# A two-layer mixture of experts on one core: weighting expert 0 in the first pass of the down phase, in place of the second

## The chip, the core and the metric

The kernel runs on one core of a Trainium2 chip. TensorE (PE) multiplies matrices into PSUM; VectorE (DVE), ScalarE (ACT) and GpSimd (POOL) work beside it, and DMA queues of SyncE (SP) and POOL move data between HBM and SBUF. Every engine takes its instructions in order. The metric is the time of one execution on the device in microseconds.

## The reference

Three stages follow one another: an attention, a mixture of experts with one expert a token, and a second mixture in which all eight experts see every token and their results are added, weighted with a matrix P. The change touches only the last product of the third stage.

```python
def _moe2_ref(x, w_gate, w1, w2):          # N, D, E, F = 2304, 512, 8, 1024
    logits = x @ w_gate
    logits = logits - logits.max()
    P = np.exp(logits)
    for _ in range(8):
        P /= P.sum(1, keepdims=True) + 1e-09
        P /= P.sum(0, keepdims=True) + 1e-09
        P *= N / E
    out = np.zeros((N, D), dtype=np.float32)
    for e in range(E):
        h = np.maximum(x @ w1[e], 0.0)
        ye = h @ w2[e]
        out += P[:, e:e + 1] * ye
```

## The kernel before

The third stage has an up phase (x @ w1) and a down phase (h @ w2). Both cut their matrices into 2 x 2 quadrants and form the product from seven block products instead of eight, on sums and differences of quadrants. Blocks are numbered b = 0 to 6. For h the seven operands are: b 0 is h11, b 2 is h12 - h11, b 3 is h22 - h12, b 1 is h22 - h12 + h11, b 4 is h21, b 6 is h22, and b 5 is h21 less the operand of b 1. An operand in float32 is split into a rounded part (a cast on ACT, L939) and the remainder (a subtraction on DVE, L943), and a block product consists of three products of these parts.

The tokens are taken in NU = 3 parts of UN = 384 (times two for the quadrants). In the up phase `up` (L1143 ff.) multiplies the quadrants of h by P for the experts 1 to 7, combines them and saves the seven operands in `hd[e, u, b]` in HBM. For expert 0 P isn't known yet at that time (it is computed while expert 0 runs), so its four quadrants are saved unweighted in the places of b 0, 2, 4 and 6.

The down phase is one loop over 168 products n. Its order is the table `STEPS`: two passes (experts 1, 2, 3, 4, then 5, 6, 7, 0), in each the blocks in the order 0, 3, 1, 2, 4, 6, 5, in each block the four experts, and for each of these the three parts u. So a pass has 84 products, and a block round has 12. Expert 0 is last of its round, but in block 5 of the second pass it is first. A product is 24 matmuls of 128x384 (L1446) into the PSUM bank of its part; after the fourth expert of a round, DVE adds the bank into the quadrants of the result (`merge`, one to four additions of 128x768, at most two of them a product). Tile names: `df` holds four stages of 768 KB for h and some W2 quadrants, `xa` and `w1c` the rounded parts and remainders, `dg`, `wr` and the pad of `x` (x2) the other W2 quadrants, `pbx` rows of P; `rA` to `rD` are the four banks, `kept` is the identity.

What is issued behind the matmuls of product n, in this order:

- `h_make(n + 3)`: the operand of the product three further on is cast and split; then `h_load` asks SP for the next stages. For expert 0 `h_make` also loads a second block (`SRC`) into the next stage, combines the two on DVE (L1325, L1331, L1333), multiplies by P (L1328, `p_load` fetches P), and in four blocks stores what later blocks need (L1335, from POOL's queue).
- `w_make(m + 1)`, once in three products: a sum of two W2 quadrants on DVE for the blocks 3, 1, 2 and 6, then its cast and its remainder.
- merges, then the loads of W2 quadrants (`w_load`).

In block 5 of the second pass finished rows leave as well: `put` transposes them on PE (L1399) into a bank, ACT copies them, and POOL writes them out by an indirect DMA (L1404).

Of the kernel before, what the change touches and what calls it, by code (L numbers as in the profile page):

```python
# [97 lines left out]
def _program(ctx, tc, qT, kT, vv, tau, wg, mod, mbias, cst, wA, wg2, wU, wD, out):  # L98
# [678 lines left out]
    def experts(es):  # L777
# [450 lines left out]
        def gates():  # L1228
# [21 lines left out]
        PASS = ((1, 2, 3, 4), (5, 6, 7, 0))  # L1250
        DORD = (0, 3, 1, 2, 4, 6, 5)
        STEPS = [(i, b, e) for i, es4 in enumerate(PASS) for b in DORD
                 for e in (es4 if (i, b) != (1, 5) else es4[3:] + es4[:3])]
        NM = len(STEPS)
        SEQ = [(m, u) for m in range(NM - 2) for u in range(NU)] + [(m, u) for u in range(NU) for m in (NM - 2, NM - 1)]
        NB = len(SEQ)
        SRC = {0: (0,), 3: (6, 2), 1: (3, 0), 2: (2, 0), 4: (4,), 6: (6,), 5: (4, 1)}
        LOADS = [(n, b) for n, (m, u) in enumerate(SEQ)
                 for b in (SRC[STEPS[m][1]] if STEPS[m][2] == 0 else STEPS[m][1:2])]
        FIRST = {}  # L1260
        for i, (n, _) in enumerate(LOADS):
            FIRST.setdefault(n, i)
        SCALED = [n for n, (m, u) in enumerate(SEQ) if STEPS[m][2] == 0 and STEPS[m][1] in (0, 3, 2, 4, 6)]
        NST = 4
        loaded = [0]

        def open_down():
            xb_s.close()
            df = es.enter_context(pool_l("df")).tile([P, N_X], F32, name="df")
            D["stage"] = [cut(df, N_T * i, 4, UN) for i in range(NST)]  # L1270
            D["w"] = [[cut(xa, 2048 * j + 1024 * i, 4, 256) for i in range(2)] for j in range(2)]
            D["h"] = [[cut(t, lo + N_T * i, 4, UN) for i in range(2)]
                      for t, lo in ((xa, 4096), (xa, 4096 + 2 * N_T), (w1c, 0), (w1c, 2 * N_T))]
            at = NST * N_T
            D["blk"] = {(j, 0): cut(df, at + 1024 * j, 4, 256) for j in range(4)}
            D["o"] = [cut(df, at + 1024 * i, 2, 512) for i in range(4)]

        def open_rest():
            xc_s.close()
            dg = es.enter_context(tc.tile_pool(name="dg", bufs=1, side="right", reuse_waits="tile")).tile(  # L1280
                [P, N_X], F32, name="dg")
            room = [cut(dg, 1024 * i, 4, 256) for i in range(10)] + [cut(wr, 0, 4, 256), pad]
            D["blk"].update(((j, i), room.pop(0)) for i in (2, 3, 1) for j in range(4))

        def w_load(i, j, k):
            nc.sync.dma_start(out=D["blk"][j, k],
                              in_=wD[PASS[i][j], :, 1024 * k:1024 * k + 1024].rearrange("p (k n) -> p k n", k=4))

        def w_make(m):
            if m >= NM:  # L1290
                return
            i, b, e = STEPS[m]
            j = PASS[i].index(e)
            w11, w12, w21, w22 = (D["blk"][j, k] if (j, k) in D["blk"] else None for k in range(4))
            if b == 3:
                op2(V, w21, w11, w21, ALU.subtract)
            elif b == 1:
# [1 line left out]
            elif b == 2:  # L1299
                op2(V, w11, w21, w11, ALU.add)  # L1300
            elif b == 6:
                op2(V, w12, w12, w21, ALU.subtract)
            both(D["w"][m % 2], {0: w11, 3: w21, 1: w21, 2: w11, 4: w12, 6: w12, 5: w22}[b], A, V)

        def h_load(n):
            top = FIRST.get(n, len(LOADS)) + NST
            while loaded[0] < min(top, len(LOADS)):
                k, b = LOADS[loaded[0]]
                m, u = SEQ[k]
                nc.sync.dma_start(out=D["stage"][loaded[0] % NST], in_=hd[STEPS[m][2], u, b])  # L1310
                loaded[0] += 1

        def p_load(i):
            if i < len(SCALED):
                load_p(pbs[i % 2], 0, SEQ[SCALED[i]][1])
# [24 lines left out]
        for n in range(n_up):  # L1340
# [96 lines left out]
        for n, (m, u) in enumerate(SEQ):  # L1437
# [12 lines left out]
            if m < NM - 3:  # L1450
                if u == 0:
                    w_make(m + 1)
            elif m == NM - 3:
                if u:
                    w_make(m + u)
            if last:
                merge(i, b, u, q[u][:, :, 0:UN])
            for _ in range(min(2, len(pend))):
# [3 lines left out]
            elif i == 0 and u == 2:  # L1462
                if b == 4:
                    w_load(1, j, 0)
                elif b == 5:
                    w_load(1, j, 2)
                    w_load(1, j, 1)
                    if j == 0:
                        p_load(0)
                        p_load(1)  # L1470
            elif (i, b) == (1, 0) and u == 2:
                w_load(1, j, 3)
            if (i, b) == (1, 5):
# [112 lines left out]
```

## Time and profile before

| | us |
|---|---|
| runs shown (3) | 2038.81, 2039.24, 2040.8; median 2039.24 |
| profiled execution | 2038.46 |
| its span, first to last instruction | 2036.7 |
| PE busy in the span | 1982.0 |
| DVE busy in the span | 1555.2 |
| down phase, first product to last instruction | 1294.4 to 2036.7 |

The times of the profile count from the span's start. A matmul that stands in the queue behind another counts as busy PE, so the length of a stretch against the number of products in it says more than PE's busy share. The granted clock of TensorE is given as a share of full speed (2.4 GHz); the lower level is 1.2 GHz. The first product of the second pass, number 84, starts at 1643.85 us.

### The profile page before, as it was taken

To read this page: it belongs to the slowest core of one execution; us is meant where nothing else is said; L and a number is where in the kernel's file an instruction comes from. 1 tells how busy PE (TensorE), PEld (TensorE's weight loads), DVE (VectorE), ACT (ScalarE), POOL (GpSimd) and SP (SyncE) were. 2 spreads that over 40 slices of the span, in tenths; PEclk is the share of its full clock that TensorE was granted. 3 is DMA by queue.
4 is the path that set the end of the run, shared out by engine and by line. 5 is a ranking of instruction groups with operands and counts; after the bars stand their busy time and mean duration, and the time that the engine had idled before them with its cause. 6 is when DMAs were issued, how large, how long until landed. Compare 5 with 4: busy or idle time off the path is not lost.

```text
span 2036.7 us, 32533 instructions
## 1 busy us (share of the span) xinstructions
PE 1982.0 (97%) x12677; PEld 1906.8 (94%) x12677; DVE 1555.2 (76%) x1957; ACT 870.6 (43%) x1152; POOL 483.7 (24%) x395
## 2 busy tenths in 40 slices
PE   8999998999998999999999999999999999999997
PEld 7877777999978999999999999999999999989997
DVE  7888886656566799999999999867766568778772
ACT  6777763555554322222222222454444443334433
POOL 6564625042002133323233323100000000000004
PEclk9999998999999999999999999999999999999999
DMA  5232324566523566677767676985565777767763
GB/s 188 84 123 100 100 66 155 194 224 198 187 92 107 177 236 233 230 254 252 242 232 238 228 251 235 398 300 188 186 212 205 256 269 257 277 238 255 260 228 120
DMA packets 177215, 421.13 MB, mean 207 GB/s; under 512 B 16396, under 2 KB 126364, under 8 KB 177052
## 3 DMA queue, kind: packets, MB, share of 16 engines
q1 hardware_dynamic: 170700, 399.03, 56.8%
q0 software_dynamic: 4928, 19.93, 2.6%
q8 instruction: 102, 1.67, 0.3%
q14 instruction: 61, 0.50, 0.1%
q10 hardware_dynamic: 1424, 0.01, 0.0%
HBM read 274.91 MB, written 143.99 MB: 206 GB/s over the span
## 4 chain that ended last, share of the span: by engine, by line
PE 58%; issue 7%; DVE 2%; ACT 1%; DMA 1%; POOL 0%; POOLq 0%; ACTq 0%; DVEq 0%; SPq 0%
PE qB L1136 10%; PE qC L1136 10%; PE qA L1136 9%; PE rA L1446 7%; PE rD L1446 6%; PE rB L1446 6%; PE rC L1446 6%; PE qD L1136 4%; DVE df L946 1%; ACT xa L939 1%; DVE xa L943 1%; DMA df<-hd 0%; DMA hd<-df 0%; ACT w1c L939 0%; DVE x L946 0%
## 5 line engine op out<-in xcount | busy, mean ns | idle before, releaser
L943 DVE TENSOR_TENSOR xa<-df,xa 128x1536 fp32r<-128x1536 f32 (+1 forms) x100 | 166.2, 1670 | 88.8 <-ACT xa L939 88.7
L946 POOL TENSOR_TENSOR x<-x 128x768 f32<-128x768 f32 x45 | 115.0, 2555 | 443.2 <-DVE x L1140 349.5
L939 ACT CAST xa<-df 128x1536 fp32r<-128x1536 f32 (+1 forms) x100 | 139.9, 1412 | 156.1 <-DVE df L946 66.2
L943 DVE TENSOR_TENSOR w1c<-df,w1c 128x1536 fp32r<-128x1536 f32 x84 | 147.4, 1756 | 72.1 <-ACT w1c L939 70.3
L946 DVE TENSOR_TENSOR x<-x 128x768 f32<-128x768 f32 x135 | 196.3, 1454 | 4.5
L939 ACT CAST w1c<-df 128x1536 fp32r<-128x1536 f32 x84 | 124.4, 1482 | 160.2 <-DVE df L946 55.8
L1335 POOL DMA_DIRECT2D hd<-df x12 | 6.6, 549 | 594.3 <-DVE df L946 594.3
L1136 PE MATMUL qB<-xc,w1c 128*128 128x384 f32 x768 | 143.7, 335 | 2.9 <-DVE x L946 1.9
L1136 PE MATMUL qC<-xa,w1c 128*128 128x384 f32 x768 | 144.0, 335 | 1.5 <-ACT x L1192 1.5
L1136 PE MATMUL qA<-xb,w1c 128*128 128x384 f32 x768 | 144.4, 336 | 0.2 <-ACT x L1192 0.2
L478 DVE TENSOR_REDUCE cols<-s 128x1 f32<-128x576 f32 x144 | 103.9, 754 | 44.6 <-PE s L473 43.6
L1136 PEld LDWEIGHTS qB<-xc,w1c 128*128 128x128 f32 x768 | 133.9, 188 | 3.5 <-issue 2.2
L1136 PEld LDWEIGHTS qA<-xb,w1c 128*128 128x128 f32 x768 | 134.5, 189 | 2.8 <-issue 2.2
L1136 PEld LDWEIGHTS qC<-xa,w1c 128*128 128x128 f32 x768 | 133.7, 188 | 1.8 <-ACT x L1192 1.8
L489 ACT ACTIVATE sa<-s,cols 128x576 f32<-128x576 f32 x144 | 102.6, 741 | 64.2 <-DVE cols L478 64.1
L1140 DVE SCALAR_TENSOR_TENSOR x<-x,pbx 128x768 f32<-128x768 f32 x126 | 125.8, 999 | 4.3
L473 PE MATMUL s<-colr 128*128 128x288 f32 x640 | 107.2, 309 | 6.5 <-DVE cols L500 2.5
L172 DVE TENSOR_TENSOR colr<-cols,colr 128x1024 fp32r<-128x1024 f32 x57 | 71.5, 1258 | 54.7 <-ACT colr L171 54.5
L473 PEld LDWEIGHTS s<-colr 128*128 128x128 f32 x640 | 88.9, 189 | 16.4 <-issue 10.7
L1446 PE MATMUL rA<-xa 128*128 128x384 f32 x576 | 104.0, 335 | 0.0
L946 DVE TENSOR_TENSOR x<-qD,x 128x768 f32<-128x768 f32 x84 | 80.0, 952 | 31.2 <-ACT x L1186 16.8
L1446 PE MATMUL rD<-w1c,xa 128*128 128x384 f32 x552 | 101.2, 338 | 0.0
(299 smaller groups left out, 4460.3 us busy)
## 6 DMA issues: line engine op xcount, KB each, us to landing
df<-hd SPq DMA_DIRECT2D x180, 768.0 KB, 4.5
hd<-x SPq DMA_DIRECT2D x317, 384.0 KB, 3.2
cols<-wA SPq DMA_DIRECT2D x84, 512.0 KB, 4.5
pbx<-pd SPq DMA_DIRECT2D x114, 192.0 KB, 5.3
wr<-wU SPq DMA_DIRECT2D x16, 768.0 KB, 6.2
dg<-wD SPq DMA_DIRECT2D x20, 512.0 KB, 6.9
hd<-df POOLq DMA_DIRECT2D x12, 768.0 KB, 7.3
cols<-qT SPq DMA_DIRECT2D x15, 576.0 KB, 3.8
```

Of the source, the lines that this page charges most:

```text
L172: sub.tensor_tensor(out=lo[i], in0=raw, in1=hi[i].bitcast(F32), op=ALU.subtract)
L473: mm(s[:, hf, 0:288], lhsT=l, rhs=r, start=n == 0, stop=n == len(ops) - 1)
L478: V.tensor_reduce(out=mx[:, i % 18:i % 18 + 1], in_=St[i][:, :, 0:288], axis=AX.XY, op=ALU.max, negate=True)
L489: A.activation(out=e.rearrange("p (h c) -> p h c", h=2), in_=St[i][:, :, 0:288], func=AF.Exp, bias=mxs[i // 18 % 2][0][:, i % 18:i % 18 + 1])
L939: A.copy(out=out, in_=in_)
L943: sub.tensor_tensor(out=hi_lo[1], in0=src, in1=hi_lo[0].bitcast(F32), op=ALU.subtract)
L946: eng.tensor_tensor(out=out, in0=x, in1=y, op=op)
L1136: mm(q[:, i, 0:UN], lhsT=a[l][:, k, 128 * i:128 * i + 128], rhs=b[r][:, k], start=first and k == 0 and j == 0, stop=k == nk - 1 and j == 2 ...
L1140: V.scalar_tensor_tensor(out=out, in0=src, scalar=0.0, in1=bc(pv.unsqueeze(1), [P, n, UN]), op0=ALU.max, op1=ALU.mult)
L1335: G.dma_start(out=hd[0, u, b], in_=x)
L1446: mm(q[u][:, i2, 0:UN], lhsT=a[l][:, k, 128 * i2:128 * i2 + 128], rhs=h[r][:, k], start=first and k == 0 and j == 0, stop=last and k == 3 ...
```

## The change

Expert 0 is no longer weighted and combined when its operands are due. A new function, `weigh0(n)`, does so in the first pass, in 12 groups of six products (n = 12 to 83): a group takes one part u and one of the four column blocks k of a quadrant (128x384, 192 KB). It loads the four quadrants in its first two products (SP), multiplies them by P, forms the combinations, eight DVE operations in its fourth, fifth and sixth product, and stores the seven operands from POOL's queue. Its five small tiles `D["p"]` lie in `df`, `wr`, `pbx` (two) and `dg`. `h_make` treats expert 0 like the others; `STEPS` has it last in block 5 as well. Apart from that, the sum of W2 quadrants is taken out of `w_make` into `w_sum`, which is called at the second product of a step for the step after the next, so ahead of its cast. (A step is the three products of one expert and block.)

```diff
-                 for e in (es4 if (i, b) != (1, 5) else es4[3:] + es4[:3])]
+                 for e in es4]
...
+            D["p"] = [df[:, at + 4096:at + 4096 + UN], wr[:, 1024:1024 + UN], pbs[1][0], pbs[1][1]]
...
+            D["p"].append(dg[:, 10240:10240 + UN])
...
         def h_make(n):
             if n < NB:
-                m, u = SEQ[n]
-                _, b, e = STEPS[m]
-                x = D["stage"][FIRST[n] % NST]
-                if e == 0:
-                    y = D["stage"][(FIRST[n] + 1) % NST]
-                    if b == 3:
-                        op2(V, x, x, y, ALU.subtract)
-                    if n in SCALED:
-                        i = SCALED.index(n)
-                        op2(V, x, x, bc(pbs[i % 2][0 if b in (0, 4) else 1].unsqueeze(1), [P, 4, UN]), ALU.mult)
-                        p_load(i + 2)
-                    if b == 1:
-                        op2(V, x, x, y, ALU.add)
-                    elif b in (2, 5):
-                        op2(V, x, x, y, ALU.subtract)
-                    if b in (0, 3, 1, 4):
-                        G.dma_start(out=hd[0, u, b], in_=x)
-                both(D["h"][n % 4], x, A, V)
+                both(D["h"][n % 4], D["stage"][n % NST], A, V)
                 h_load(n + 1)
+
+        def weigh0(n):
+            gr, s = divmod(n - 12, 6)
+            if not 0 <= gr < 4 * NU:
+                return
+            u, k = divmod(gr, 4)
+            h11, h12, h21, h22, t1 = D["p"]
+            pv = pbs[0]
+            src = lambda b: hd[0, u, b, :, k]
...
+            def scale(x, t, b=None):
+                op2(V, x, x, pv[t], ALU.mult)
+                if b is not None:
+                    G.dma_start(out=src(b), in_=x)
+
+            def comb(out, x, y, op, b):
+                op2(V, out, x, y, op)
+                G.dma_start(out=src(b), in_=out)
+
+            if s == 0:
+                if k == 0:
+                    load_p(pv, 0, u)
+                load(h12, 2)
+                load(h22, 6)
+            elif s == 1:
+                load(h11, 0)
+                load(h21, 4)
+            elif s == 3:
+                scale(h11, 0, 0)
+                scale(h12, 1)
+                comb(t1, h12, h11, ALU.subtract, 2)
+            elif s == 4:
+                scale(h22, 1, 6)
+                comb(h12, h22, h12, ALU.subtract, 3)
+            elif s == 5:
+                comb(h11, h12, h11, ALU.add, 1)
+                scale(h21, 0, 4)
+                comb(t1, h21, h11, ALU.subtract, 5)
...
             if m < NM - 3:
                 if u == 0:
                     w_make(m + 1)
+                elif u == 1:
+                    w_sum(m + 2)
             elif m == NM - 3:
                 if u:
                     w_make(m + u)
+            weigh0(n)
```

On DVE, three places show what moved. The first is the end of block 1's round in the first pass, products 33 to 35. Before (L943 of 128x1536 is the remainder of h, with which a product's list begins; 128x1024 is W2, `x_3583` the merges):

```order
L943 TENSOR_TENSOR xa<-df,xa 128x1024
L946 TENSOR_TENSOR x_3583<-rC,x_3583 128x2x384 x2
L943 TENSOR_TENSOR xa<-df,xa 128x1536
L946 TENSOR_TENSOR x_3583<-rC,x_3583 128x2x384
L946 TENSOR_TENSOR x_3583<-rB,x_3583 128x2x384
L943 TENSOR_TENSOR w1c<-df,w1c 128x1536
L946 TENSOR_TENSOR x_3583<-rB,x_3583 128x2x384 x2
```

And now, at the same place:

```order
L943 TENSOR_TENSOR xa<-df,xa 128x1024
L946 TENSOR_TENSOR df<-df,pbx 128x384
L946 TENSOR_TENSOR wr<-wr,pbx 128x384
L946 TENSOR_TENSOR dg<-wr,df 128x384
L946 TENSOR_TENSOR x_3583<-rC,x_3583 128x2x384 x2
L943 TENSOR_TENSOR xa<-df,xa 128x1536
L946 TENSOR_TENSOR df<-dg,df 128x1024
L946 TENSOR_TENSOR pbx<-pbx 128x384
L946 TENSOR_TENSOR wr<-pbx,wr 128x384
L946 TENSOR_TENSOR x_3583<-rC,x_3583 128x2x384
L946 TENSOR_TENSOR x_3583<-rB,x_3583 128x2x384
```

Ahead of the merges stand three operations of expert 0 in one product, and a W2 sum and two operations in the next.

The second place is in the second pass, expert 0 in block 3, the W2 sum of the block that follows among its rows. Before:

```order
L946 TENSOR_TENSOR df<-df 128x1536
L946 TENSOR_TENSOR df<-df,pbx 128x1536
L943 TENSOR_TENSOR xa<-df,xa 128x1536
L946 TENSOR_TENSOR dg<-df,dg 128x1024
L943 TENSOR_TENSOR xa<-dg,xa 128x1024
L946 TENSOR_TENSOR df<-df 128x1536
L946 TENSOR_TENSOR df<-df,pbx 128x1536
L943 TENSOR_TENSOR w1c<-df,w1c 128x1536
```

And now the same stretch, between the last merges of block 0 and the sums for block 1:

```order
L943 TENSOR_TENSOR w1c<-df,w1c 128x1536
L946 TENSOR_TENSOR dg<-df,dg 128x1024
L943 TENSOR_TENSOR xa<-df,xa 128x1536 x2
L943 TENSOR_TENSOR xa<-dg,xa 128x1024
L943 TENSOR_TENSOR w1c<-df,w1c 128x1536
```

The combinations and multiplications of 128x1536 are gone, and the W2 sum stands two rows of h ahead of the remainder that needs it, not right ahead of it.

The third place is SP's queue in the first pass, which before held only the loads of h (L1310) there. Now a group's four loads stand among those of the other experts:

```order
L1312 DMA df<-hd 128x1536 x5
L1330 DMA wr<-hd 128x384
L1330 DMA pbx<-hd 128x384
L1312 DMA df<-hd 128x1536
L1330 DMA df<-hd 128x384
L1330 DMA pbx<-hd 128x384
```

Behind the two pairs, the experts' loads of 768 KB go on in the same queue.

## Rows read from the trace of the kernel before

**Rows 1.** The page, part 1: busy time, share of the span, instructions.

```profile
PE 1982.0 (97%) x12677; PEld 1906.8 (94%) x12677; DVE 1555.2 (76%) x1957; ACT 870.6 (43%) x1152; POOL 483.7 (24%) x395
```

**Rows 2.** Stretches of the down phase: length, busy time by engine, granted clock, DMA.

```profile
1294.41:1643.85 349.44, 349.44 (x2018) 349.44 (x2017) 232.43 (x165) 154.53 (x118) 2.56 (x1) 1.00 0.67 241
...
1697.93:1703.83 5.90, 4.32 (x25) 4.03 (x25) 4.73 (x6) 3.80 (x3) 0.00 (x0) 1.00 0.93 372
...
1741.58:1749.31 7.73, 4.44 (x24) 4.12 (x24) 4.66 (x4) 2.58 (x3) 0.00 (x0) 1.00 0.91 299
1749.31:1755.15 5.84, 5.84 (x25) 5.84 (x25) 5.84 (x6) 2.63 (x2) 0.00 (x0) 0.71 0.76 290
...
1796.75:1805.95 9.20, 4.38 (x25) 4.06 (x24) 4.57 (x4) 2.56 (x3) 0.00 (x0) 0.91 0.78 268
1805.95:1812.60 6.65, 6.64 (x24) 6.64 (x25) 6.65 (x7) 4.28 (x3) 0.00 (x0) 0.61 0.93 358
...
1845.88:1857.91 12.03, 8.78 (x49) 8.14 (x48) 8.73 (x7) 2.99 (x3) 0.00 (x0) 1.00 0.60 220
1857.91:1863.78 5.87, 5.87 (x24) 5.87 (x25) 5.87 (x5) 3.65 (x3) 0.00 (x0) 0.71 0.72 263
...
1967.78:1974.26 6.48, 4.33 (x25) 4.00 (x24) 4.86 (x5) 3.89 (x4) 0.00 (x0) 1.00 0.64 243
1974.26:1980.93 6.67, 6.67 (x32) 6.67 (x33) 6.16 (x4) 3.87 (x4) 2.58 (x4) 0.74 0.96 350
```

**Rows 3.** Timeline, start and length in us; in brackets idle time before and releaser.

```profile
1793.27 1.76 DVE L946 TENSOR_TENSOR df<-df 128x1536 f32<-128x1536 f32 x1 [3.01 <-DMA df<-hd]
1795.14 1.48 ACT L939 CAST w1c<-df 128x1536 fp32r<-128x1536 f32 x1 [6.67 <-DVE df L946]
...
1800.09 1.47 ACT L939 CAST xa<-df 128x1536 fp32r<-128x1536 f32 x1 [3.47 <-DMA df<-hd]
...
1803.27 1.22 DVE L946 TENSOR_TENSOR df<-dg,df 128x1024 f32<-128x1024 f32 x1
...
1805.95 6.81 PE L1446 MATMUL rC<-xa 128*128 128x384 f32 x24 [4.82 <-ACT xa L939]
```

**Rows 4.** Groups of DVE in the down phase: busy us, mean ns | idle before.

```profile
L943 DVE TENSOR_TENSOR w1c<-df,w1c 128x1536 fp32r<-128x1536 f32 x84 | 147.4, 1756 | 72.1 <-ACT w1c L939 70.3 <-PE rD L1446 1.6 <-PE rA L1446 0.2
...
L946 DVE TENSOR_TENSOR df<-df,pbx 128x1536 f32<-128x1536 f32 x15 | 26.3, 1754 | 0.1
L946 DVE TENSOR_TENSOR df<-df 128x1536 f32<-128x1536 f32 x12 | 21.0, 1753 | 3.1 <-DMA df<-hd 3.0
L946 DVE TENSOR_TENSOR x<-rB,x 128x768 f32<-128x768 f32 x20 | 18.6, 953 | 6.3 <-PE rB L1446 6.2
```

**Rows 5.** Groups of DVE in the whole span, the forms nearest to 128x384.

```profile
L946 DVE TENSOR_TENSOR x<-x 128x768 f32<-128x768 f32 x135 | 196.3, 1454 | 4.5
...
L943 DVE TENSOR_TENSOR w1c<-wr,w1c 128x512 fp32r<-128x512 f32 x75 | 51.7, 689 | 15.4 <-ACT w1c L939 15.4
...
L811 DVE SCALAR_TENSOR_TENSOR late<-p,late 128x256 fp32r<-128x256 f32 x80 | 32.9, 420 | 29.7 <-ACT late L810 29.4
```

**Rows 6.** DMA: two stretches; landing of POOL's stores, and of P's loads from 1862 us.

```profile
1400.00:1500.00 100.00, 100.00 (x579) 100.00 (x578) 73.39 (x55) 44.82 (x34) 0.00 (x0) 1.00 0.55 191
...
1862.00:1920.00 58.00, 58.00 (x335) 58.00 (x335) 46.51 (x35) 26.06 (x20) 1.70 (x4) 1.00 0.85 298
...
DMA to landing us min/median/max: 4.0/7.3/9.6
...
pbx<-pd SPq DMA_DIRECT2D x6, 192.0 KB, 6.5
```

**Rows 7.** POOL's issues of the output, duration ns least, median, most.

```profile
L1404 POOL DMA_INDIRECT out<-df,kept x18: 965/966/2461, 1976.9 to 2030.5; - x18
```

**Rows 8.** PE's timeline at the first put; the chain of work at another.

```profile
1974.26 1.32 PE L1399 MATMUL rC<-kept,x 128*128 128x128 f32 x8 [2.16 <-DVE x L946]
...
2003.68 0.87 PE rC L1399 x8
```

More of the change, by code (lines that the diff above doesn't have):

```diff
@@ L1256, in experts @@
         NB = len(SEQ)
[L1257 to L1263, printed above, removed]
         NST = 4
@@ L1287, in w_load, with blocks, w_sum @@
                               in_=wD[PASS[i][j], :, 1024 * k:1024 * k + 1024].rearrange("p (k n) -> p k n", k=4))
-        def w_make(m):
+        def blocks(m):
+            i, b, e = STEPS[m]
+            j = PASS[i].index(e)
+            return i, b, (D["blk"][j, k] if (j, k) in D["blk"] else None for k in range(4))
+        def w_sum(m):
             if m >= NM:
                 return
-            i, b, e = STEPS[m]
-            j = PASS[i].index(e)
-            w11, w12, w21, w22 = (D["blk"][j, k] if (j, k) in D["blk"] else None for k in range(4))
+            i, b, (w11, w12, w21, w22) = blocks(m)
             if b == 3:
@@ L1302, in w_make @@
                 op2(V, w12, w12, w21, ALU.subtract)
+        def w_make(m):
+            if m >= NM:
+                return
+            i, b, (w11, w12, w21, w22) = blocks(m)
             both(D["w"][m % 2], {0: w11, 3: w21, 1: w21, 2: w11, 4: w12, 6: w12, 5: w22}[b], A, V)
         def h_load(n):
[L1306 to L1310, printed above, removed]
+            while loaded[0] < min(n + NST, NB):
+                m, u = SEQ[loaded[0]]
+                _, b, e = STEPS[m]
+                nc.sync.dma_start(out=D["stage"][loaded[0] % NST], in_=hd[e, u, b])
@@ L1311, in h_load @@
                 loaded[0] += 1
-        def p_load(i):
-            if i < len(SCALED):
-                load_p(pbs[i % 2], 0, SEQ[SCALED[i]][1])
         def h_make(n):
             if n < NB:
-                m, u = SEQ[n]
-                _, b, e = STEPS[m]
-                x = D["stage"][FIRST[n] % NST]
-                if e == 0:
-                    y = D["stage"][(FIRST[n] + 1) % NST]
-                    if b == 3:
-                        op2(V, x, x, y, ALU.subtract)
-                    if n in SCALED:
-                        i = SCALED.index(n)
-                        op2(V, x, x, bc(pbs[i % 2][0 if b in (0, 4) else 1].unsqueeze(1), [P, 4, UN]), ALU.mult)
-                        p_load(i + 2)
-                    if b == 1:
-                        op2(V, x, x, y, ALU.add)
-                    elif b in (2, 5):
-                        op2(V, x, x, y, ALU.subtract)
-                    if b in (0, 3, 1, 4):
-                        G.dma_start(out=hd[0, u, b], in_=x)
-                both(D["h"][n % 4], x, A, V)
-                h_load(n + 1)
+                both(D["h"][n % 4], D["stage"][n % NST], A, V)
@@ new lines, in h_make, with load @@
+                h_load(n + 1)
+        def weigh0(n):
+            gr, s = divmod(n - 12, 6)
+            if not 0 <= gr < 4 * NU:
+                return
+            u, k = divmod(gr, 4)
+            h11, h12, h21, h22, t1 = D["p"]
+            pv = pbs[0]
+            src = lambda b: hd[0, u, b, :, k]
+            def load(x, b):
+                nc.sync.dma_start(out=x, in_=src(b))
+            def scale(x, t, b=None):
[24 more added lines that the diff above has]
+                comb(t1, h21, h11, ALU.subtract, 5)
@@ L1467, in experts @@
                     w_load(1, j, 1)
-                    if j == 0:
-                        p_load(0)
-                        p_load(1)
             elif (i, b) == (1, 0) and u == 2:
```

## The prediction

> **What bounds the kernel now.** I read first the page's busy shares: PE is busy 97% of the span [rows 1], so only places where PE stands still can give anything back. Then I cut the down phase into stretches by the starts of PE's products (a product is the 24 matmuls of one step n, 0 to 167) and read each stretch's length, PE count and granted clock [rows 2]. The first pass, products 0 to 83, takes 349.44 us: 84 x 4.16 us, with no gap at all. So 4.16 us is the pitch, and the first pass is at PE's floor. In the second pass seven stretches are too long. Excess over 4.16 us a product: 1.74 (5.90), 3.57 (7.73), 1.68 (5.84), 5.04 (9.20), 2.49 (6.65), 3.71 (12.03 for two), 1.71 (5.87). Together **19.94 us**. Near the end come 6.48 for one product (2.32 over) and 6.67 for one product and a put's eight transposes, 0.87 us in the chain of work [rows 8] (1.64 over): **3.96 us** more.
>
> There are two kinds among these. In the stretches 5.90, 7.73, 9.20, 12.03 and 6.48 PE stands idle at a granted clock of 0.91 to 1.00. In the stretches behind them (5.84, 6.65, 5.87, 6.67) PE is busy throughout, at a mean granted clock of 0.61 to 0.74: part of the time on the lower level, 1.2 GHz, after the idle time. These 1.7 to 2.5 us are a second price of the same gaps and go with them.
>
> Who is late? The timeline of the 9.20 us stretch [rows 3] shows one product of expert 0: DVE waits 3.01 us for a transfer, combines (1.76), ACT has idled 6.67 us when it may cast, DVE makes the rest; the next cast waits 3.47 us for its transfer; then DVE forms a sum of W2 blocks (1.22), ACT casts it only behind that, and PE waits 4.82 us for this cast. Transfer, combination, sum of W2 and cast stand in one line, only for expert 0. In the 6.48 us stretch the put's transposes wait for a merge [rows 8] that is behind expert 0's combination of block 5 in DVE's queue.
>
> **The change part by part.**
>
> *Removed, second pass.* 15 multiplications by P and 12 combinations of 128x1536, 27 x 1.75 us [rows 4] = 47.4 us of DVE; the second load of a pair (12 x 768 KB), the 12 stores, and 30 loads of P less the 6 of the new place. Expert 0 is then like the other experts: one load, one cast, one subtraction a product. What is late next? The heaviest place left is the first block of the pass, with 12 merges of 0.95 us in six steps: a step costs DVE 1.76 (subtraction) + 1.91 (two merges) + about 0.81 (the W2 work of 2.44 us every third step or split over two) = 4.48 against 4.16, so DVE falls behind by 2 us over six steps; its work is issued three products ahead, up to 12.5 us. The 1.74 us in front of product 97 go too: there PE waits for a bank, and the first bank's four merges now end within one product and a half, and its next use is four products on. I count all seven excesses, 19.94 us, as gone.
>
> *The order in block 5 and the put.* Expert 0 goes from first to last there and needs no combination; the merge that the put waits for has only a subtraction ahead of it (1.76 us). 3.96 us gone.
>
> *Sums of W2 two steps ahead.* 1.22 us each, no more work, moved two products earlier: the cast finds it done. It costs nothing by itself and flattens DVE's lists: the heavy first product of a step loses 1.22, the second gains it.
>
> *Added, first pass.* 96 DVE operations of 128x384, eight in a group of six products. Their price isn't in the trace. The neighbours: 0.42 (128x256) and 0.69 (128x512) [rows 5]; I take 0.55, the middle, so 52.8 us. The far bound is the 128x768 form between two SBUF tiles, which took 1.45 on average instead of 0.95 while POOL ran tensor work: the same stretch makes 0.55 into 0.84. A gain is excluded, since nothing is taken from DVE there. Does it fit? DVE's list at the busiest place, products 33 to 38 (nine merges and the last half of a group; its rows stand with the change): 33: 1.76 + 1.22 + 3 x 0.55 + 1.91 = 6.5; 34: 1.76 + 1.22 (sum) + 1.1 + 1.91 = 6.0; 35: 1.76 + 1.65 + 1.91 = 5.3; 36: 1.76 + 1.22 + 1.91 = 4.9; 37: 3.9; 38: 1.8. W2's remainder costs 1.22 like its sum [rows 3]. A list begins with its product (0.3 us for the hand-over, my estimate) or when the one before ends, so they end 6.8, 8.7, 9.8, 10.5, 10.3 and 7.9 us after the start of their own product. The latest thing that PE needs is the W2 remainder of list 36, done 8.6 us after the start; PE needs it at 12.5. Spare 3.9 us; with 0.84 an operation 1.6. So **0 us** on the path; what hides it is the three products of lead. A whole round of 12 products there holds 12 x 1.76 + 8 x 1.22 + 9 x 0.95 = 39.5, and 16 x 0.55 with it makes 48.3 of 49.9 us: nearly full, which is the weak point.
>
> *Added transfers.* 48 loads and 84 stores of 192 KB, 26 MB in 300 us: 87 GB/s on top of 191 at a share of 0.55. Stretches of 298 GB/s had a share of 0.85 and no excess but the clock's [rows 6]; I expect 0.75 to 0.85, and about 1 in the last block of the pass, where eight W2 loads join. POOL, empty till now in this phase, issues the stores in order; SP's loads for expert 0 wait for stores of the group before, with the experts' 768 KB loads queued behind them. Those run four products ahead (16.6 us), so SP may wait some 8 us at no cost. DVE itself waits at the sixth product of a group until the stores of its fourth have landed, 8.3 us later by the program; behind it stand the subtraction and merges of the next list. The nearest rows: 768 KB from POOL landed in 4.0, 7.3, 9.6 us (least, median, most), 192 KB of P in 6.5 [rows 6]. A quarter of the bytes speaks for the lower half; I take 4 to 6, which is hidden, and keep 9.6 for the range.
>
> *POOL's issue.* The output's issues at the end took 0.97 to 2.46 us [rows 7]; beside a busy DVE I bound a store's issue by the longest. Seven at 2.46 are 17 of a group's 25 us: they fit, but each store starts up to 1.5 us later than at 0.97. By the Trainium skill ("SBUF — State Buffer", section "Who interferes with whom") tensor_tensor with both inputs in SBUF contends only with GpSimd's reads, and a store's descriptors would not be held up by it; the trace doesn't settle it, since these issues are indirect ones. By that page the delay is nil, by the row 1.5 us, and the sum is the same.
>
> **Sum.** 2038.46 (profiled execution) - 19.94 - 3.96 + 0 = 2014.56 us; span 2012.8. The median of the runs, 2039.24, is 0.8 above the profiled one: **2015.3 us**.
>
> **The rivals.**
>
> *A, slower: expert 0's buffers go round too slowly.* In a group h11 is scaled, stored (landing L), overwritten by the combination once that has landed, stored again (L), loaded anew once that has landed (L), scaled. Three landings, three operations and three issues: 2.6 + 3L us, against 25.0 us for a group. Up to L = 7.5 us nothing happens; beyond it each of the 12 groups stalls DVE, then PE. It costs more than it gains from 12 x (2.6 + 3L - 25) - 8 (lead) = 24, L = 8.4 us; with POOL 1.5 us late at both stores, 7.4. At 9.6 in every group it costs 69: 2015 + 69 = **2084 us**; at 9.0, 47: 2062; just beyond the turning point, some 2045. For it: 7.3 median on POOL, and a share near 1 late in the pass. Against: the 9.6 is the slowest of twelve stores of four times the size. Chance 0.12.
>
> *B, the gain comes in part: DVE is the bound of the first pass.* At 0.84 an operation a round holds 39.5 + 13.4 = 52.9 of 49.9 us at its fullest, and single waits for landings eat the rest of the lead: four to eight stalls of 1 to 3 us, each followed by 1.7 us on the lower clock. 6 to 18 us back: **2021 to 2033 us**. For it: the full round; against: the neighbours' emptier lists. Chance 0.18.
>
> *C, it doesn't do what it says.* The excesses are due to the merges and casts, and only transfers are spared: then the 19.94 us stay, and only the put's 3.96 may go: **2035 to 2041 us**. Against: the first pass has the same merges and casts and no gap, and in the four longest stretches the late ones are expert 0's. Chance 0.05.
>
> **How the numbers follow.** The forecast, 2013 to 2019, has 0.65. Low end: nothing more than the 23.9 is there to go, and runs differ by 1 to 2 us: 2013. The high end takes in B up to 2033; A and C are left out, with 0.17. About 0.2% (4 us) is what a measurement of this kernel can tell from no change. Faster: 0.65 + 0.18 = 0.83; within 0.2%: 0.05, C; slower: 0.12, A.
>
> **What would show it.** Right: PE's starts 4.16 us apart from product 0 to the puts, in both passes; no granted clock below 1.0 between them; DVE 80 to 97% busy from 1344 to 1644 us; operations of 128x384 at 0.5 to 0.6 us; the second pass's DVE without 1.75 us multiplications. Wrong in the step on transfers: DVE waiting at a 128x384 subtraction for "DMA hd<-" and PE gaps every 25 us. Wrong in the step on DVE: PE waiting for "xa" or "w1c" around products 33 to 39, with DVE never idle. Wrong about the cause: excesses left in the second pass.

## The result, and the profile after

| | before | changed |
|---|---|---|
| median of the runs, us | 2039.03 (2037.22 to 2040.8, 4 runs) | 2014.65 (2010.66 to 2015.4, 4 runs) |
| profiled execution, us | 2038.46 | 2015.4 |
| its span, us | 2036.7 | 2013.6 |

The ratio is 0.9877, with a 95% interval of 0.9859 to 0.9894. 2015.3 us were forecast, with a range of 2013 to 2019.

The page of the changed kernel, part 1 (busy us, share of the span, instructions), answers to [rows 1]:

```profile
PE 1973.7 (98%) x12677; PEld 1900.8 (94%) x12677; DVE 1556.0 (77%) x2026; ACT 872.2 (43%) x1152; POOL 523.4 (26%) x467
```

DVE's busy time is that of before within 1 us: the work on expert 0 has moved from one pass to the other, it has not become less. Stretches of the changed kernel (length; busy PE, PEld, DVE, ACT, POOL; granted clock; DMA share; GB/s), the first pass, the second up to the first put, and the puts, answer to [rows 2]:

```profile
1297.35:1646.79 349.44, 349.44 (x2017) 349.44 (x2017) 277.35 (x261) 154.71 (x118) 46.87 (x84) 1.00 0.88 314
1646.79:1950.40 303.61, 303.61 (x1753) 303.61 (x1753) 208.65 (x155) 132.17 (x99) 1.14 (x3) 1.00 0.58 203
1950.40:2005.00 54.60, 54.13 (x338) 53.39 (x336) 19.21 (x13) 20.09 (x18) 20.86 (x28) 1.00 0.40 139
```

The first pass took 349.44 us, exactly as before, though DVE had 277 us of work in it in place of 232 and the DMA engines moved 314 GB/s in place of 241. In the second pass PE was busy for all of its 303.61 us, at full clock. Every stretch over 4.16 us a product is gone. One wait is left in the down phase. PE's timeline (start, length, in brackets idle time before and its releaser), its first product and the last two transposes of the last put but one (one more put of eight follows at once):

```profile
1297.35 4.32 PE L1468 MATMUL rA<-xa 128*128 128x384 f32 x24
...
2003.61 0.44 PE L1421 MATMUL rB<-kept,x 128*128 128x128 f32 x2 [0.40 <-DVE x L946]
```

Between these two starts lie 706.26 us; before it was 730.48 (1294.41 to 2024.89), so the change took 24.22 us off. Two other differences lie outside: product 0 started 2.94 us later in this execution, and from those transposes to the end of the span it took 9.99 us in place of 11.81. -24.22 + 2.94 - 1.82 gives the 23.1 us between the spans.

### The profile page after: what moved, and what is told of

Same layout as the page of the kernel before. It is cut to its first block, busy times and chain, and to the rows that moved or that the text cites. A ratio compares the mean times of both kernels' runs of the same rounds, so it can differ in the third digit from the quotient of the medians.

```text
span 2013.6 us, 32801 instructions
## 1 busy us (share of the span) xinstructions
PE 1973.7 (98%) x12677; PEld 1900.8 (94%) x12677; DVE 1556.0 (77%) x2026; ACT 872.2 (43%) x1152; POOL 523.4 (26%) x467
## 4 chain that ended last, share of the span: by engine, by line
PE 68%; DVE 0%; POOL 0%; ACT 0%; issue 0%; POOLq 0%; ACTq 0%
PE qB L1136 10%; PE qC L1136 10%; PE qA L1136 9%; PE rD L1468 9%; PE rA L1468 9%; PE rB L1468 8%; PE rC L1468 8%; PE qD L1136 4%; PE rC L1421 0%; POOL out L1426 0%; DVE x L946 0%; DVE pbx L1111 0%; PE rB L1421 0%; POOLq L1604 0%; ACT df L1423 0%
## 5 line engine op out<-in xcount | busy, mean ns | idle before, releaser
L943 DVE TENSOR_TENSOR xa<-df,xa 128x1536 fp32r<-128x1536 f32 (+1 forms) x100 | 166.2, 1670 | 86.9 <-ACT xa L939 86.8
L943 DVE TENSOR_TENSOR w1c<-df,w1c 128x1536 fp32r<-128x1536 f32 x84 | 147.4, 1755 | 79.2 <-ACT w1c L939 78.9
L1426 POOL DMA_INDIRECT out<-df,kept x18 | 23.1, 1285 | 337.2 <-ACT df L1423 335.1
L1468 PEld LDWEIGHTS rA<-xa 128*128 128x128 f32 x576 | 100.0, 188 | 0.0
```

What stands on the lines that cost most here:

```text
L943: sub.tensor_tensor(out=hi_lo[1], in0=src, in1=hi_lo[0].bitcast(F32), op=ALU.subtract)
L1426: ins = G.indirect_dma_start(out=out, in_=o[:, h], in_offset=None, out_offset=bass.IndirectOffsetOnAxis(ap=idx_c[:, i:i + 1], axis=0))
L1468: mm(q[u][:, i2, 0:UN], lhsT=a[l][:, k, 128 * i2:128 * i2 + 128], rhs=h[r][:, k], start=first and k == 0 and j == 0, stop=last and k == 3 ...
```

## The experiments

The start of product 0 differs by up to 6 us between the profiled executions (1293.4 to 1299.2), so the kernels are compared by the **stretch** from there to the two transposes named above, beside their times. Each ratio is to runs of the kernel before that were taken beside it (their medians lie between 2038.7 and 2039.9 us).

| kernel | stretch, us | median, us | ratio (95%) |
|---|---|---|---|
| before | 730.48 | 2039.03 | |
| changed | 706.26 | 2014.65 | 0.9877 (0.9859 to 0.9894) |
| no_weigh | 706.26 | 2016.66 | 0.9888 (0.9872 to 0.9904) |
| order_back | 706.26 | 2013.45 | 0.9872 (0.9857 to 0.9887) |
| sums_late | 706.78 | 2013.16 | 0.9869 (0.9854 to 0.9884) |
| stores_aside | 706.26 | 2018.23 | 0.9900 (0.9885 to 0.9916) |
| dve_twice | 712.65 | 2019.32 | 0.9907 (0.9891 to 0.9924) |
| sums_only | 712.85 | 2018.44 | 0.9904 (0.9883 to 0.9926) |
| sum_first | 715.57 | 2023.47 | 0.9933 (0.9917 to 0.9949) |
| one_load | 720.45 | 2029.25 | 0.9946 (0.9929 to 0.9963) |
| groups_of_4 | 723.15 | 2032.08 | 0.9970 (0.9957 to 0.9984) |
| rest_late | 728.61 | 2038.87 | 0.9997 (0.9989 to 1.0006) |
| stores_twice | 839.43 | 2150.60 | 1.0539 (1.0516 to 1.0563) |

### Is the added work free? (no_weigh)

```diff
-                 nc.sync.dma_start(out=D["stage"][loaded[0] % NST], in_=hd[e, u, b])
+                 nc.sync.dma_start(out=D["stage"][loaded[0] % NST], in_=hd[e, u, {1: 0, 3: 6, 5: 4}.get(b, b) if e == 0 else b])
...
-             weigh0(n)
```

> The changed kernel without the work of weigh0: expert 0 is neither multiplied by P nor combined, in no pass, and its operands of the blocks 1, 3 and 5 are read from the quadrants that lie stored. So 96 operations of 128x384, 48 loads and 84 stores are left out, nothing else. My theory: all of that work lies behind PE, so this kernel takes as long as the changed one, 2014.65 us within 2 us, with no PE wait between product 0 and the puts in either. Rival: the added work still costs something on the path (an earlier stage's transfers, the put, the end), then this one is at 2011 us or below. Second rival: expert 0's work was never the cause of the gaps, then gaps remain here too, at 2020 us or above.

The stretch was 706.26 us, to the hundredth that of the changed kernel. 96 DVE operations, 132 transfers and the six loads of P that go with them cost nothing on the path. (The median was 2 us higher, within the spread of its five runs, 2011.68 to 2018.53.)

### Which part brings the gain? (sums_late, sums_only, order_back, one_load)

The changed kernel with the sums back where they were:

```diff
         def w_make(m):
...
+            w_sum(m)
...
-                elif u == 1:
-                    w_sum(m + 2)
```

> The changed kernel with the sums of W2 blocks put back: each is formed right ahead of its cast, in the first product of the step before, instead of two products earlier. My theory: the early sums gain little or nothing by themselves, but the lists of DVE at the end of block 1 in the first pass get one wait longer (sum 1.22, cast 1.05 on ACT, remainder 1.22 in one row): by my count the W2 remainder of product 36 is then done 12 us after the product's start, of 12.5 allowed. So 2014.7 to 2018 us, with at most one or two PE waits near 1447 us. Rival: the sums were half of the gain, as the timeline of the 9.20 us stretch could be read (sum and cast stand right ahead of PE's 4.82 us wait): then 2022 us or above, with gaps in the second pass.

The changed kernel with the old order of block 5:

```diff
-                 for e in es4]
+                 for e in (es4 if (i, b) != (1, 5) else es4[3:] + es4[:3])]
```

> The changed kernel with expert 0 first again in block 5 of the second pass. My theory: it was the combination on DVE ahead of the merge that made the first put wait, and the order doesn't matter once there is no combination: 2014.65 us within 2 us, no PE wait at the first put. Rival: it was the order itself (another expert last, other buffers at the end) that freed the put: then the 3.96 us come back, 2018.6 us, with PE waiting some 2 us for DVE's merge.

The kernel before with the early sums and nothing else (`w_sum` is taken out of `w_make` as in the change):

```diff
...
             if m < NM - 3:
                 if u == 0:
                     w_make(m + 1)
+                elif u == 1:
+                    w_sum(m + 2)
```

> The kernel before with the early sums alone; expert 0 is weighted and combined in the second pass as before. My theory: the sums are the smaller part. Each of the three groups of gaps at expert 0 gets shorter by the sum that PE's cast no longer waits for, 1.2 to 2.5 us: 3 to 7 us in all, 2032 to 2036 us. Rival: the sums in front of the cast were the cause, and expert 0's work fits by itself: then below 2025 us. Other rival: the transfers end last, the sums are hidden: 2039 us within 2 us.

The kernel before without expert 0's second loads and its stores:

```diff
-         SRC = {0: (0,), 3: (6, 2), 1: (3, 0), 2: (2, 0), 4: (4,), 6: (6,), 5: (4, 1)}
+         SRC = {0: (0,), 3: (6,), 1: (0,), 2: (2,), 4: (4,), 6: (6,), 5: (4,)}
...
-                     y = D["stage"][(FIRST[n] + 1) % NST]
+                     y = x
...
-                    if b in (0, 3, 1, 4):
-                        G.dma_start(out=hd[0, u, b], in_=x)
```

> The kernel before, with expert 0's second loads and its 12 stores left out (the combination takes the one block twice, so the values are others); all 27 operations of 1.75 us on DVE stay, in their places. It parts transfers from DVE's work in the gaps of the second pass. My theory: both stand in the same line, the waits for transfers (3.01 and 3.47 us in the 9.20 us stretch) being the greater part: more than half of the 19.94 us goes, 2022 to 2030 us with the put's 3.96 us still there. Rival: DVE's operations alone make the gaps: 2034 us or above. Other rival: the transfers alone: 2019 us or below, only the put's wait left.

Moving expert 0's work, with the new order but without the early sums (sums_late), takes 23.7 us off the stretch; the order of block 5 takes nothing. Both were expected, though sums_late came 1.5 us under its range. But the sums alone (sums_only), for which the prediction had counted nothing and the expectation 3 to 7 us, take **17.6** of the 24.2 us. The two gains don't add up (41 for 24): each of the two edits, alone, breaks most of the same chain. PE's waits in the down phase, before (engine, line, waited for; us in total, times, longest):

```profile
PE rC L1446 <- ACT xa L939: 4.8, 1, 4.8
PE rB L1446 <- ACT xa L939: 3.3, 1, 3.3
PE rA L1446 <- ACT w1c L939: 2.4, 1, 2.4
PE rC L1399 <- DVE x L946: 2.2, 1, 2.2
PE rC L1446 <- DVE x L946: 1.6, 1, 1.6
```

and with the early sums alone:

```profile
PE rB L1454 <- DVE x L946: 2.0, 1, 2.0
PE rB L1454 <- ACT xa L939: 1.9, 1, 1.9
PE rB L1407 <- DVE x L946: 0.4, 1, 0.4
PE rB L1454 <- DVE xa L943: 0.3, 1, 0.3
```

The 4.8 us wait is gone, and the put's 2.2 as well, though expert 0 is still combined in the second pass and still first in block 5. The timeline of the kernel with the early sums, at the place of [rows 3], shows how:

```profile
1782.23 1.22 DVE L946 TENSOR_TENSOR df<-dg,df 128x1024 f32<-128x1024 f32 x1
...
1787.35 1.76 DVE L946 TENSOR_TENSOR df<-df 128x1536 f32<-128x1536 f32 x1 [3.90 <-DMA df<-hd]
...
1791.72 2.43 ACT L939 CAST xa<-df 128x1536 fp32r<-128x1536 f32 x2 [1.02 <-DMA df<-hd]
1793.23 2.89 DVE L943 TENSOR_TENSOR xa<-df,xa 128x1536 fp32r<-128x1536 f32 x2 [0.74 <-ACT xa L939]
...
1795.38 4.33 PE L1454 MATMUL rC<-xa 128*128 128x384 f32 x24
```

The sum of W2 (1782.23) stands ahead of DVE's wait for a transfer. That wait is even longer than before, 3.90 us for 3.01 in [rows 3], and costs PE nothing here: when the last stage of h arrives, ACT casts h and W2 in one go (x2) and DVE makes both remainders in one go. Before, the sum stood behind the wait, and cast and remainder of W2 followed it one by one.

Without the second load and the stores (one_load) 10.0 of 24.2 us come back, just over half of the 19.94, and the time lies in the range expected. The transfers are thus not the whole chain: in this kernel DVE waits for no transfer in the second pass (no idle time before its combinations but 0.1 us), and 14.2 us are still lost. What is left are waits for casts and merges behind DVE's combinations and multiplications, among them the 2.4 and 1.6 us waits and the put's, as before:

```profile
PE rA L1444 <- ACT w1c L939: 2.4, 1, 2.4
PE rB L1444 <- ACT xa L939: 2.2, 2, 1.3
PE rC L1397 <- DVE x L946: 2.1, 1, 2.1
PE rB L1444 <- ACT w1c L939: 1.7, 1, 1.7
PE rC L1444 <- DVE x L946: 1.6, 1, 1.6
```

### What about a late sum is dear? (rest_late, sum_first)

Two theories were formed on the sums. A late sum makes DVE idle for some 1.2 us, from its end to the end of ACT's cast (19.1 us of such idle time before the 23 remainders of W2 in the second pass of before, none in sums_only). Or the sum's place behind expert 0's wait is what counts. The first run makes the remainder a call, `rest`, which `w_make(m + 1, True)` returns behind sum and cast:

```diff
...
                 if u == 0:
-                    w_make(m + 1)
+                    rest = w_make(m + 1, True)
+                elif u == 1:
+                    rest()
```

> The kernel before, with one thing changed: the remainder of W2 (DVE, 128x1024) is issued one product later than its cast, behind the next product's subtraction of h. The sum stays where it was, behind expert 0's work and ahead of its cast. Theory 1, formed after the run with the early sums alone: a late sum makes DVE stand idle for about 1.2 us, from the end of the sum to the end of ACT's cast (some 19 us of such idle time in the second pass, none with early sums), and it is this idle time that empties the three products of lead; it goes here, so 2019 to 2027 us. Theory 2: what counts is the sum's place behind expert 0's wait for its transfer, which holds up the cast itself; nothing is moved there, so 2034 to 2040 us.

The second takes the sum out of `w_make`, into `w_sum`, and calls it ahead of `h_make`:

```diff
...
+            if m < NM - 3 and u == 0:
+                w_sum(m + 1)
             h_make(n + 3)
             j = m % 4
             if m < NM - 3:
                 if u == 0:
                     w_make(m + 1)
```

> The kernel before, with the sum of W2 still in the first product of a step, but issued ahead of that product's work on h, and so ahead of expert 0's wait for its transfer and of its combination. Cast and remainder stay. Theory 1 (the idle time of DVE between sum and remainder) and theory 2 (the sum's place behind the transfer) both expect it to do nearly all that the early sums do: 2017 to 2023 us. If a lead of two products is needed: 2028 us or more.

With the remainder one product later DVE's idle time ahead of it is 0.0, and next to nothing is gained (1.9 us of the stretch, none of the median). The largest group of these remainders in the second pass, before and in rest_late (busy us, mean ns | idle before), and PE's longest waits in rest_late:

```profile
L943 DVE TENSOR_TENSOR xa<-dg,xa 128x1024 fp32r<-128x1024 f32 x12 | 14.7, 1225 | 11.7 <-ACT xa L939 11.7
```

```profile
L1306 DVE TENSOR_TENSOR xa<-dg,xa 128x1024 fp32r<-128x1024 f32 x12 | 14.6, 1218 | 0.0
```

```profile
PE rC L1452 <- DVE xa L1306: 4.5, 2, 2.7
PE rB L1452 <- DVE xa L1306: 3.7, 2, 2.6
PE rA L1452 <- DVE xa L1306: 2.9, 1, 2.9
```

PE's waits for the cast shrank (to 1.8 and 1.5 us), and in their place it waits for the remainder, which now stands behind expert 0's next combination. So this run takes away one wait and makes another, and can't refute the idle time. sums_late has the same 19.1 us of idle time in the second pass, but no work on expert 0 there, and PE waits only once, 0.25 us: the idle time alone opens no gap. Whether it does beside expert 0's work, neither run shows.

Putting the sum ahead of the same product's work on h, two calls swapped, takes 14.9 of the 24.2 us. 2023.47 us are just above the 2017 to 2023 that both theories had given, so this run does not part them: it moves the sum ahead of the wait, and DVE's idle time ahead of the remainder is gone as well. The same group in sum_first:

```profile
L943 DVE TENSOR_TENSOR xa<-dg,xa 128x1024 fp32r<-128x1024 f32 x13 | 15.8, 1217 | 0.0
```

Theory 2 as it was put, the wait for the transfer, can't be all: one_load has no such wait and still loses 14.2 us. What is shown is that the order of the two calls is worth 14.9 us; how much of it is the wait, the combination in front of the sum or the idle time behind it stays open. The two products of lead in sums_only are worth 2.7 us more.

### How near are the bounds? (dve_twice, groups_of_4, stores_twice, stores_aside)

All four change the changed kernel. Each of the 96 operations of 128x384 is followed by another of the same size:

```diff
                 op2(V, x, x, pv[t], ALU.mult)
+                op2(V, x, x, x, ALU.max)
...
                 op2(V, out, x, y, op)
+                op2(V, out, out, out, ALU.max)
```

> The changed kernel with each of the 96 operations of 128x384 followed by a second one of the same cost that leaves the values as they are (the maximum of a tile and itself). It measures how near DVE is to being the bound of the first pass. By my bookkeeping a round of 12 products holds 39.5 + 32 x 0.55 = 57.1 of 49.9 us in block 1, 54.3 in the blocks 3 and 2, and less than 49.9 in the others: 16 us too much, of which the lead of three products takes some 8. So 8 us of PE waits and two or three stretches on the lower clock of 1.7 us: 2022 to 2029 us, the waits between 1394 and 1500 us and for casts or remainders. Rival: DVE has more room than that (idle time that I count as needed): 2014.7 us within 2 us.

52 us more of DVE cost 6.4 us, at one place; 2019.32 us lie between the two expectations. The 49.9 us around it, from product 31 on (1423.00 to 1472.90), PE's only gap in the first pass, and DVE's operations at it:

```profile
1423.00:1472.90 49.90, 46.76 (x253) 46.19 (x252) 49.20 (x56) 18.05 (x14) 6.47 (x12) 0.93 0.74 261
```

```profile
1455.38 7.14 PE L1470 MATMUL rB<-w1c,xa 128*128 128x384 f32 x24 [3.14 <-DVE x L946]
```

```profile
1453.42 1.81 DVE L946 TENSOR_TENSOR x<-rB,x 128x768 f32<-128x768 f32 x2
1455.15 1.75 DVE L943 TENSOR_TENSOR w1c<-df,w1c 128x1536 fp32r<-128x1536 f32 x1
1456.82 1.22 DVE L943 TENSOR_TENSOR xa<-df,xa 128x1024 fp32r<-128x1024 f32 x1
```

The place is the one that the prediction's bookkeeping had named, DVE is 49.2 of 49.9 us busy there, and rival B is thereby real; but PE waits for the merges of bank rB, not for a cast or a remainder. The product behind the gap takes 7.14 us instead of 4.32, which is the second price seen in [rows 2].

A group in four products instead of six:

```diff
-            gr, s = divmod(n - 12, 6)
+            gr, s = divmod(n - 12, 4)
+            s = (0, 1, 3, 4)[s]
...
-            elif s == 5:
```

> The changed kernel with the 12 groups of weigh0 in four products each instead of six (loads in the first and second, three operations in the third, five in the fourth), so over products 12 to 59. This tests the loop of buffers by its period, 16.6 instead of 25.0 us. With the landings measured in the changed kernel (stores 5.0 and 5.3 us, loads 6.4) one turn takes at least 2.6 + 16.7 = 19.3 us: 2.7 us over in each of 11 turns, 29 us, less the lead of some 8, and with up to ten stretches on the lower clock of 1.7 us: 2035 to 2055 us, with DVE waiting for the transfers 'hd<-' and '<-hd' and PE for the casts behind. Rival: the landings hide behind the queues' other work and only DVE's load counts (24 operations a round, 52.8 of 49.9 us in one round): 2014.7 to 2018 us.

16.9 us were lost; 2032.08 us lie between the two expectations, 3 us under the first. Expert 0's first operation comes again after 16.7 to 20.7 us, 18.5 on average, in place of 16.64. The prediction's formula with the landings of this run (4.4 us for the two stores from `df`, 6.2 for the load) gives 2.6 + 4.4 + 4.4 + 6.2 = 17.6, but the nearness of the two numbers is no proof of it. DVE waits for the load in every group; for the stores, whose landings are two of the formula's three, DVE doesn't wait at all and SP once. The waits of DVE and of SP's queue, and the first of PE's four gaps (0.6 to 3.9 us):

```profile
DVE df L946 <- DMA df<-hd: 39.2, 12, 5.5
```

```profile
SPq L1331 <- DMA hd<-wr: 0.5, 1, 0.5
```

```profile
1452.68 7.24 PE L1468 MATMUL rC<-xa 128*128 128x384 f32 x24 [3.91 <-DVE x L946]
```

The edit did something else besides: a group of six issues its last loads two products ahead of their first use, a group of four one product, 4.16 us, ahead, and the load takes 6.2 us. That is the wait seen. DVE's lists are fuller by the same edit. So the run shows the price of a load issued too late, beside fuller lists, and not that of the buffers' round trip.

Each store issued twice to the same place:

```diff
-                    G.dma_start(out=src(b), in_=x)
+                    for _ in range(2):
+                        G.dma_start(out=src(b), in_=x)
...
-                G.dma_start(out=src(b), in_=out)
+                for _ in range(2):
+                    G.dma_start(out=src(b), in_=out)
```

> The changed kernel with each of the 84 stores issued twice, to the same place: POOL's issues and the bytes it writes double (16.5 MB more in 300 us, 55 GB/s on top of 314). It asks how near the transfers are to the bound. By the loop's formula nothing happens as long as the three landings sum to less than 22.4 us (they sum to 16.7 now): with the transfers' share near 1 I expect landings of 6 to 8 us and 0.5 us more of issue a store, so 2014.7 to 2025 us, with waits of DVE for stores in many groups but few of PE. Rival: saturation lengthens the 768 KB loads beyond their lead of four products: PE waits all through the first pass, 2035 us or above. Other rival: the transfers have ample room: within 2 us of 2014.65.

It cost 133 us. By the number that is the first rival (2035 us or above), but not by its reason: the loads of 768 KB landed in 4.9 us, sooner than in the changed kernel (6.0). The edit did more than meant: in this program the second store to a place waits until the first has landed, and POOL takes its queue in order. POOL's waits in that kernel:

```profile
POOL hd L1336 <- DMA hd<-pbx: 116.1, 23, 7.4
POOL hd L1336 <- DMA hd<-df: 78.2, 12, 7.9
POOL hd L1341 <- DMA hd<-dg: 62.3, 23, 5.1
...
POOL hd L1341 <- DMA hd<-wr: 40.1, 11, 6.3
POOL hd L1341 <- DMA hd<-df: 35.7, 11, 5.8
```

332 us in 12 groups are 27.7 us a group; with 14 issues of 0.54 us that is 35.3, and the groups took 36.1 (25.0 + 133.2 / 12). A round trip above 25 us shows undiminished in the time, but this run says nothing of traffic. So the copies were sent to another place:

```diff
+    hd2 = dram.tile([NU, 7, P, 4, UN], F32, name="hd2")
...
                     G.dma_start(out=src(b), in_=x)
+                    G.dma_start(out=hd2[u, b, :, k], in_=x)
...
                 G.dma_start(out=src(b), in_=out)
+                G.dma_start(out=hd2[u, b, :, k], in_=out)
```

> The changed kernel, with a second copy of each of the 84 stores of 192 KB to another place in HBM that nobody reads. Unlike the second store to the same place, it need not wait for the first to land. It adds 16.5 MB in 300 us, 55 GB/s, and 84 issues of POOL of 0.54 us. Theory 1: the 136 us of the doubled stores came from the landings that POOL's queue had to wait for between the two stores of a pair; here no such wait, landings rise from 5.2 us to below the 7.5 us at which the round trip of the buffers binds, so 2013 to 2024 us. Theory 2: the transfers themselves were at their limit (share 0.88 to 0.95 in the first pass), and any further bytes stretch the landings beyond 7.5 us: 2045 us or more.

Theory 1 holds: the stretch is 706.26 us, no gap. Its first pass, columns as above:

```profile
1296.57:1646.01 349.44, 349.44 (x2018) 349.44 (x2018) 275.61 (x258) 154.86 (x118) 88.52 (x163) 1.00 0.96 356
```

and three rows of its transfers from 1330 to 1660 us (KB each, median us to landing):

```profile
df<-hd SPq DMA_DIRECT2D x79, 768.0 KB, 7.1
hd<-df POOLq DMA_DIRECT2D x48, 192.0 KB, 6.2
hd<-pbx POOLq DMA_DIRECT2D x48, 192.0 KB, 7.5
```

At a share of 0.96 the landings reach the 7.5 us of the turning point. Here the round trip begins to bind: SP's loads wait 43.0 us in all for the landing of stores (1.5 in the changed kernel) and DVE 9.7 (none there). The largest of each:

```profile
SPq L1331 <- DMA hd<-pbx: 17.5, 9, 2.5
```

```profile
DVE dg L947 <- DMA hd<-dg: 8.0, 5, 2.1
```

PE sees nothing yet. Its median is 3.6 us above the changed kernel's; in the profiled execution the difference lies behind the last output, in the last section.

## Why the prediction was right, and where it was not

**The size of the gap** was right: 23.90 us were counted from the stretches, waits and the lower clock behind them together; 24.22 went. The tail gave 1.8 us more and the earlier stages took 2.9; the prediction had neither, and that they nearly cancel is luck. The step that booked the gaps on expert 0's work was right as well: moving that work without the early sums (sums_late) takes 23.7 us.

**The cause was told in one part too few.** The step "It costs nothing by itself and flattens DVE's lists" sized the early sums at zero. On top of expert 0's move that held (0.5 us, sums_late against the changed kernel), but alone they were worth 17.6 us. The chain was read rightly from [rows 3] (transfer, combination, sum of W2, cast), but all of it was booked on expert 0, because it was late only there. A chain of four links that has just too little lead is broken by shortening it at either end. Had the change consisted of the sums alone, the same working would have said "no change" and been wrong by some 20 us. Rival C's excesses did not stay: the second pass of the changed kernel has none.

**Order in block 5:** the 3.96 us went, but not through the order; order_back has neither the gap nor the lower clock. In the trace of before two steps of expert 0 follow each other there (end of block 6, start of block 5), and DVE ends the put's merge 6.4 us after the start of the product beside it; with the early sums alone, in the same order, it is 4.0 us, and the wait is gone. So DVE's backlog out of block 6 is what the two traces differ in; the order would count only in as far as it lengthened that.

**Added DVE work.** 0.55 us was estimated for 128x384; the groups of the changed kernel in the first pass have means of 552 to 558 ns, none near the 0.84 of rival B:

```profile
L946 DVE TENSOR_TENSOR pbx<-pbx 128x384 f32<-128x384 f32 x24 | 13.3, 552 | 0.0
L946 DVE TENSOR_TENSOR wr<-pbx,wr 128x384 f32<-128x384 f32 x12 | 6.7, 558 | 0.4
...
L946 DVE TENSOR_TENSOR df<-df,pbx 128x384 f32<-128x384 f32 x12 | 6.7, 554 | 0.8 <-DMA df<-hd 0.8
```

In DVE's queue they cost less than the 52.8 us of that sum. Its busy time in the first pass grew from 232.43 to 277.35 us, by 0.47 us an operation: in list 33 an operation that doesn't need the result of the one before starts 0.47 us behind it (1437.77 and 1438.24 us), one that does 0.59 (1438.83). In 50 us windows between 1344.7 and 1646.8 us DVE was 74 to 88% busy, where 80 to 97% had been named as a sign.

The lists 33 to 36 ended 6.5, 7.9, 8.7 and 9.1 us after the start of their product (6.8, 8.7, 9.8 and 10.5 were worked out), and the remainder of W2 in list 36 at 7.3:

```profile
1449.83 1.81 DVE L946 TENSOR_TENSOR x<-rB,x 128x768 f32<-128x768 f32 x2
1451.56 1.75 DVE L943 TENSOR_TENSOR w1c<-df,w1c 128x1536 fp32r<-128x1536 f32 x1
1453.23 1.22 DVE L943 TENSOR_TENSOR xa<-df,xa 128x1024 fp32r<-128x1024 f32 x1
```

One thing in that step was wrong: the remainder isn't what PE needs soonest. The merges of rB at the end of list 35 are (1449.83, done at 1451.64): product 38 needs that bank, and it was there that dve_twice opened a gap. Their spare is 12.5 - 8.7 = 3.8 us by the run, 2.7 by the prediction's own figures, not the 3.9 it gave.

**Transfers.** Landings of 4 to 6 us were expected and 5.0 to 5.3 came as the median, 9.8 at most; the share was 0.88 over the first pass, for 0.75 to 0.85. DVE's waits for the loads were 0.8 us in all, SP's for the stores 1.5. Rival A did not come. stores_aside bears out its turning point in part: at landings of 6.2 to 7.5 us the waits for stores begin, and PE has no gap. What happens beyond it no run shows cleanly: groups_of_4 waits for a load issued later, and stores_twice for POOL's queue.

**POOL's issue** was bounded by the longest output issue, 2.46 us [rows 7]. That row is another kind of transfer. The stores, beside a busy DVE, with the landings of their line below:

```profile
L1335 POOL DMA_DIRECT2D hd<-pbx x24: 539/539/542, 1368.6 to 1646.8; - x24
L1335 POOL DMA_DIRECT2D hd<-df x12: 539/539/744, 1364.2 to 1638.3; - x12
...
DMA to landing us min/median/max: 2.7/5.0/9.3
```

0.54 us, at most 0.74. That agrees with the statement of the Trainium skill ("SBUF — State Buffer", "Who interferes with whom") which the prediction had set against the row.

## What to carry to other kernels

When two queues hand work to each other and only one customer is late, list every link of the chain and ask of each what taking it out alone would do: here two edits of very different size each did most of it (23.7 and 17.6 of 24.2 us), and swapping two calls (the operation that is ready ahead of the work on h that may wait for a transfer) gave 15. Check the lead of each thing that PE needs, banks as well as operands, since the tightest decides when load is added. The lead of a load counts in the same way: issued two products ahead of its use it cost DVE 0.8 us in twelve groups, one product ahead 39.2, and there, with DVE's lists fuller too, the stretch took 16.9 us more.

## What the runs showed of the hardware

The DMA engines at a mean share of 0.96 and 356 GB/s over 349 us (stores_aside) left this pipeline without a gap of PE; the small stores' median landings, tile by tile, rose from 4.4 to 5.3 us (share 0.88) to 6.2 to 7.5.

The time between the start of the last issue of the output and the end of the span goes with how many stores POOL had issued in the down phase, and not evenly: 5.2 to 5.3 us with none (one_load, no_weigh), 6.1 to 6.2 with 12 (before, sums_only, sum_first, rest_late), 4.3 to 4.4 with 84 (changed kernel, order_back, sums_late, dve_twice, groups_of_4), 10.3 with 168 (stores_aside, stores_twice alike). What happens there no row shows. In stores_aside it is 5.9 us more than in the changed kernel, which covers the 3.6 us between their medians; of the 23.1 us between the spans of before and changed it makes 1.8.
